# Two masks moved to the start of VectorE's queue, a margin on operand readiness, and a refitted order of issue, in a sliding-window attention plus mixture-of-experts kernel

## The chip, the cores and the metric

The kernel runs on one core of one Trainium2 chip. The metric is the device time of one execution in microseconds (us). The engines are named as in the profile: PE is TensorE's matmul, PEld its weight load, DVE is VectorE, ACT is ScalarE, POOL is GpSimd, SP is SyncE (here it only issues DMAs).

## The reference, cut to what matters

```python
# q, k, v: (B, H, S, D) = (4, 8, 768, 64); n_sink = 4, window = 128
scores = q @ k.T / sqrt(D)
rel = pos[:, None] - pos[None, :]
keep = (pos[None, :] < n_sink) | ((rel >= 0) & (rel < window))
a = softmax(where(keep, scores, -1e9));  attn = a @ v
x = attn.transpose(0, 2, 1, 3).reshape(3072, 512)
p = domain_probs / (domain_probs.sum(-1, keepdims=True) + 1e-9)   # (3072, 4)
out = sum over e in 0..3 of p[:, e:e+1] * (relu(x @ w1[e]) @ w2[e])  # w1: 512 x 1024, w2: 1024 x 512
```

## The kernel before

**Work.** Tokens are handled in 12 pairs of 128-row blocks: batch `b` in 0..3, group `g` in 0..2 (256 rows). Attention for (b, g) has one step per head pair `hp` in 0..3: transposes of q and k (batch 0 on PE, later batches by transposing DMAs on SP's queue), `scores` (L713; it uses 64 rows of the array, two heads side by side), exponentials on ACT (L753), a multiplication by a 0/1 mask on DVE (L734, L763), `values` (L788 for the sink keys, L795 for the window), a reciprocal and a scaling (L822, L825, L834), and for batch 0 a transpose back (`turn`, L856).

The experts' first layer comes in two forms. The dense one (L1109) is 4 groups of 8 matmuls for a unit (b, g, e). The fast one (L1192) is a Strassen-like scheme of seven products P1 to P7, which needs combinations of the tokens (`T`, L1161) and of the weights (L401 to L407), and additions between products on DVE (L1242, L1257) and ACT (L1235, L1248). ReLU and gate are applied by DVE (L1226). The second layer is dense for the first two pairs of batch 0 (`second`, L1436) and also a seven-product scheme for the other ten (`product`, L1361), which needs combinations `S` of the hidden rows (L1307, L1286, called chores) and of `w2` (L366 to L372).

**Order.** There is one instruction stream for each engine, and its order is worked out while the program is built, by a planner inside the kernel function. It keeps a clock for each engine (`t`), predicted ready times for each operand, and a list `pend` of deferred work of ACT, DVE and POOL: `later(engine, ready, slack, run)` puts work there, and among what is ready the one with the earliest `ready + slack` is issued. In each turn of the main loop PE's next step is chosen from `opts`, a list of (ready time, priority, kind):

```python
r, _, kind, step = min(opts, key=lambda o: (o[0] > now + 40, o[0] if o[0] > now + 40 else 0, o[1]))
```

So among the steps that are ready by now + 40 ns the lowest priority number wins, and if none is ready the one that is ready first. If nothing is ready within 220 ns, a product of zeros is issued as a filler (`idle_products`, L581). The priorities: an attention step 0 if due, else 3 (0.1 less for a pair of scores); a fast or dense first-layer step 2 and a little more for the second open unit; opening a unit `OPEN`; a dense second step 1 or `LOW_SECOND`; a product `HIGH_PRODUCT` if DVE's backlog in the planner's clock is over `BEHIND`, else `LOW_PRODUCT`. `SHARE_OF` and `LEAD` say when an attention step is due and when the next batch's attention begins. `LATE1` and `LATE` are added to the time at which a transposing DMA is taken to have landed (batch 1, other batches). `GATE0`, `GATE`, `FORM`, `FORM2`, `TOKEN0`, `TOKEN` are slacks of deferred work, `MARGIN` shortens that of the chores, `WAIT1` and `WAIT2` delay the weights' combinations, `CHORES` is how many chores may be in `pend` at once. `ONLY2` is the first batch for which scores that can come in pairs come only in pairs. `GROW` is the time at which `gates_by_row` (L459 to L465: four DVE operations and a DMA on SP's queue that writes normalised gates to DRAM) is issued. At most `NH` = 6 hidden tiles are live (`mix.live`).

**The masks.** `lent[:, 5*P:10*P]` holds two bias tiles `low` (0 or -32768): the first made by DVE (L536 to L540), the second by ACT (L541, L542). The bias form serves group 0 of batch 0 directly, as an accumulated matmul (L707). The 0/1 masks `mask0` (128 x 384) and `mask1` (128 x 256) are made from them by one DVE `tensor_scalar` each (L550), put into `pend` by `make_mask` with ready time 12000 and slack 8000; `mask_one` (L761) is their first user. The chores of the first product pair wait until the four stores of the dense pairs (`self.stored`) are done in the planner's clock, because `S` reuses the tiles that these stores read.

Of the kernel before, what the change touches and what calls it, by code (L numbers as in the profile page):

```python
# [9 lines left out]
ALU = mybir.AluOpType  # L10
# [6 lines left out]
def kernel(  # L17
# [12 lines left out]
    nc = tc.nc  # L30
# [7 lines left out]
    P = 128  # L38
# [23 lines left out]
    DENSE = 2  # L62
    NT3 = 3
    MIX = 4
    SHARE_OF = (0.712, 1.17, 0.907)
    LEAD = (1.333, 0.307)
    DUE = 0
    LOW_PRODUCT = 2.643
    LOW_SECOND = 4.19
    HIGH_PRODUCT = 0.939  # L70
    EARLY = 0.062
    GATE = 4459
    GATE0 = 1390
    FORM = 17347
    FORM2 = 18856
    TOKEN0 = 0
    WAIT2 = 15161
    WAIT1 = 5608
    LATE3 = 3
    TOKEN = 18312  # L80
    MARGIN = 1544
    FULL = 7
    STEP0 = 0.165
    READY = 54
    WIDE = 2
    OPEN = 1.956
    ONACT = 1
    ONE = 2
    PAIR = 1
    MASKD = 99999999  # L90
    GROW = 29126
    ONLY2 = 2
    BEHIND = 1333
    CHORES = 1
    OWN = 2
    BIASED = 1
    FAST = tuple(START)
# [7 lines left out]
    t = {"pe": 1200.0, "act": 0.0, "dve": 0.0, "pool": 1280.0, "sp": 800.0, "sw": 6500.0, "hw": 0.0}  # L105
    ring, whole = [0.0] * 6, [False] * 6
    WARM = 6600.0
    FLIP = 315
    LATE = 744
    LATE1 = 9766  # L110

    def pe(cols, *deps, n=1, switch=0):
        t["pe"] = max([t["pe"], *deps])
# [11 lines left out]
    def dve(cols, *deps, rate=0.96, fixed=157, shared=None):  # L125
        at = max([t["dve"], *deps])
        if rate == 1.92 if shared is None else shared:
            at += max(0.0, port["pool"] - at - 78)
            port["dve"] = at + fixed + cols / rate
        t["dve"] = at + fixed - 85 + cols / rate  # L130
        return at + fixed + 35 + cols / rate
# [28 lines left out]
    def later(engine, ready, slack, run):  # L160

        pend.append((ready, ready + slack, engine, run))
# [138 lines left out]
    first = {name: sb.tile([P, 2, H, D], BF16, name="qkn", tag="qkn", bufs=NQB) for name in "qk"}  # L301
# [195 lines left out]
    for h in range(H):  # L497
        r = 32 * (h // 2) + NSINK * (h % 2)
        nc.sync.dma_start(
            out=vsf[r:r + NSINK, :, 0:D], in_=v[:, h, 0:NSINK, :].rearrange("b j d -> j b d"),  # L500
# [3 lines left out]
    for sgn in (1, -1):  # L504
        nc.gpsimd.affine_select(
            out=identf, in_=identf, compare_op=ALU.is_ge, fill=0.0,
# [5 lines left out]
    for base, sgn in ((0, 1), (NSINK - 1, -1)):  # L512
        nc.gpsimd.affine_select(
            out=sel2, in_=sel2, compare_op=ALU.is_ge, fill=0.0, base=base,
# [10 lines left out]
    for i in range(1, 4):  # L525
# [7 lines left out]
    two = own[:, None, :].to_broadcast([P, 2, P])  # L533
    LOW = 32768.0
    low = [lent[:, 5 * P:8 * P], lent[:, 8 * P:10 * P]]
    nc.vector.tensor_scalar(  # L536
        out=low[0].rearrange("p (n q) -> p n q", n=3)[:, 0::2], in0=two, scalar1=LOW, scalar2=-LOW, op0=ALU.mult, op1=ALU.add,
# [4 lines left out]
    nc.scalar.activation(out=low[1][:, P:2 * P], in_=own, func=AF.Copy, scale=LOW, bias=-LOW)  # L542
    mask0 = consts.tile([P, 3 * P], BF16, name="mask0")
    mask1 = consts.tile([P, 2 * P], BF16, name="mask1")
    made = []

    def make_mask(i):
        def run(engine):
            x = (mask0, mask1)[i]
            nc.vector.tensor_scalar(out=x, in0=low[i], scalar1=1 / LOW, scalar2=1.0, op0=ALU.mult, op1=ALU.add)  # L550
            dve(4 * P)
            made.append(i)
        later("dve", 12000.0, 8000, run)

    for i in range(2):
        make_mask(i)
    t["dve"] = t["act"] = 4600.0
    cast_first(0)
    flush(4700.0)
# [10 lines left out]
        nc.vector.memset(half[64 * ph:64 * ph + 64, ph:ph + 1], 1.0)  # L570
    for x in ksd:
        nc.vector.memset(x, 0.0)
    t["dve"] += 400.0
    cast_first(1)

# [118 lines left out]
    def scores(b, hp, g, more=False):  # L694
        T = qkT[b]
        w = sum(x[2] for x in GROUPS[g]) * P
        ready = 0.0 if more else scores_ready(b, hp, g)
        slots, sps = [], []
        for ph in range(2):
            i = pick()  # L700
            slots.append(i)
            sps.append(bank(i, [P, 2 * G], FP32, "sps"))
            ring[i] = 1e12
        biased = b == 0 and g < BIASED
        if biased:
            for ph in range(2):
                nc.tensor.matmul(sps[ph][:, 0:w], lhsT=ident, rhs=low[min(g, 1)], start=True, stop=False, skip_group_check=True)  # L707
            pe(2 * w, ready, n=2)
        c = 0
        for (kb, qb, nq) in GROUPS[g]:  # L710
            for ph in range(2):
                pr = slice(64 * ph, 64 * ph + 64)
                nc.tensor.matmul(  # L713
                    sps[ph][:, c:c + nq * P],
                    lhsT=T[pr, 1, hp, kb * P:(kb + 1) * P],
                    rhs=T[pr, 0, hp, qb * P:(qb + nq) * P],
                    start=not biased, stop=True, skip_group_check=biased,
                )
            c += nq * P
        scored_at[b] = done = pe(w, ready, n=6, switch=0 if more else 2)  # L720
        a = sb.tile([P, 2, w], BF16, name="aT", tag="aT", bufs=4)
        m = mask0 if g == 0 else mask1

        def masked(at):
            aT_at[b, hp, g] = at

        if b == 0:
            part = join(2, masked)
        else:
            def mask_both(at):  # L730
                def run(engine):
                    n = 2 if g == 0 else 4
                    x = a if g == 0 else a.rearrange("p h (n w) -> p (h n) w", n=2)
                    nc.vector.tensor_mul(x, x, m[:, None, :].to_broadcast([P, n, 2 * w // n]))  # L734
                    masked(dve(2 * w, rate=1.92))

                def select(engine):
                    x = a.rearrange("p h (n k q) -> p h n k q", n=2, k=2)
                    for k, sgn in ((0, -1), (1, 1)):
                        nc.gpsimd.affine_select(  # L740
                            out=x[:, :, :, k], in_=x[:, :, :, k], compare_op=ALU.is_ge, fill=0.0,
                            base=min(sgn, 0), pattern=[[0, 2], [0, 2], [sgn, P]], channel_multiplier=-sgn,
                        )
                        at = pool(0, fixed=640, shared=True)
                    masked(at + 60)
                if g == 0 or max(t["dve"] - at, 0.0) + 500 * sum(x[2] == "dve" and x[0] < at + 300 for x in pend) < MASKD:
                    later("dve", at, 1500, run)
                else:
                    later("pool", at, 1500, select)
            part = join(2, mask_both)  # L750
        for ph in range(2):
            def run(engine, ph=ph):
                nc.scalar.activation(out=a[:, ph], in_=sps[ph][:, 0:w], func=AF.Exp, scale=scale)  # L753
                at = act(w)
                take(slots[ph], at)
                if b or biased:
                    part(at)
                    return
                assert len(made) == 2

                def mask_one(engine):  # L761
                    x = a[:, ph].rearrange("p (n w) -> p n w", n=2)
                    nc.vector.tensor_mul(x, x, m[:, None, :].to_broadcast([P, 2, 2 * P]))  # L763
                    part(dve(w, rate=1.92))
                later("dve", at, 300, mask_one)
            later("act", done, 300 + 10 * ph, run)
        aTs[b, hp, g] = a
# [700 lines left out]
    mix = Mixture()  # L1468
    att = Attention(0)
# [3 lines left out]
    ahead, upto, loaded, wide = 0, 0.0, 0, 0  # L1473
# [23 lines left out]
    while mix.more() or att.more():  # L1497
        now = t["pe"]
# [19 lines left out]
        x = next((x for x in loads if load_ready(x) < now + 1500), None)  # L1518
# [3 lines left out]
        if turns and (ahead < 2 or not mix.second) and landed.get(("qk", *turns[0]), 1e12) < now and (turns[0][0] <= ahead or turns[0][0] == ahead + 1 and not att.todo):  # L1522
            x = turns.pop(0)
# [10 lines left out]
        next_form()  # L1534
        if ahead + 1 < B and not att.more() and (ahead == 0 or (ahead + 1, 0) in turned_at) and (ahead == 0 or mix.done >= sum(work[:ahead]) * LEAD[ahead - 1]):
            ahead += 1
            att = Attention(ahead)
            upto = mix.done
        share = (sum(work[:ahead]) - upto) * SHARE_OF[max(ahead - 1, 0)]
        due = ahead == 0 or att.steps * share <= (mix.done - upto) * att.total  # L1540
        opts = []
        if att.more():
            opts = [(max(r, now), (DUE if due else 3) - 0.1 * (step == "two"), "att", step) for r, step in att.options()]
        s2, p = mix.second_ready(), mix.product_ready()
        behind = max(t["dve"] - now, 0.0) + 500 * sum(x[2] == "dve" and x[0] < now + 300 for x in pend)
        opts.append((max(p, now), HIGH_PRODUCT if behind > BEHIND or mix.live >= FULL else LOW_PRODUCT, "product", None))
        opts += [(max(f, now), p, "first", x) for f, p, x in mix.firsts()]
        opts.append((max(s2, now), 1 if mix.since >= 1 else LOW_SECOND, "second", None))
        soonest = min(o[0] for o in opts)
        if soonest > now + 40 and flush(soonest, True):  # L1550
            continue
# [3 lines left out]
        if soonest > 1e11:  # L1555
            if loads:
                x = loads.pop(0)
# [4 lines left out]
        r, _, kind, step = min(opts, key=lambda o: (o[0] > now + 40, o[0] if o[0] > now + 40 else 0, o[1]))  # L1562
# [45 lines left out]
```

## Time and profile before

| what | value |
|---|---|
| median of 3 runs | 361.19 us (361.15 to 361.68) |
| the profiled execution: its own time | 362.95 us |
| its span, first to last instruction | 361.2 us |
| granted TensorE clock | 1.000 |
| PE, DVE, ACT, POOL busy | 351.9, 308.8, 169.6, 68.6 us |
| instructions of PE, DVE, ACT, POOL | 4680, 704, 429, 90 |
| fillers (L581), warm-up ones included | 24 |

How to read it: a matmul record includes the pipeline's fill, so "PE busy" says that something was in the array, not that the array was full. Start times of successive matmuls tell more. "Idle before" is the time in which an engine had nothing running ahead of an instruction, with what ended it. The chain is followed back from the last instruction, at each step to what released it.

### The profile page before, as it was taken

Reading aid. Unit: us, or ns where it says so; the run is one execution under the profiler, and the core shown is the slowest. Engines: PE = TensorE matmul, PEld = TensorE weight load, DVE = VectorE, ACT = ScalarE, POOL = GpSimd, SP = SyncE. Lnnn points to the kernel's source line nnn. Section 1 sums busy time; section 2 is a strip of 40 time slices with the busy share of each in tenths; the row PEclk is TensorE's granted clock in tenths of the full one; section 3 lists DMA queues with packets and bytes.
Section 4 is the critical chain, followed back from the end, with each engine's and each line's share of the span. In section 5 each row is a group of like instructions: output and inputs, shape, how many; then the busy total and the mean of one; then the engine's idle time right before and its main releaser. Section 6 shows DMA issues by size and latency. Waiting matters only on the chain.

```text
span 361.2 us, 11129 instructions
## 1 busy us (share of the span) xinstructions
PE 351.9 (97%) x4680; PEld 302.7 (84%) x4680; DVE 308.8 (85%) x704; ACT 169.6 (47%) x429; POOL 68.6 (19%) x90
## 2 busy tenths in 40 slices
PE   8899999999989999999999999999999999999995
PEld 4585788767667999998998998899899999999984
DVE  5869899996979899898898899799898999979740
ACT  5764551567756531536655633952865213222110
POOL 8934015121620712010030610000000000000000
PEclk9999999999999999999999999999999999999999
DMA  9999999999990998661549999131124112000011
GB/s 176 186 193 206 220 222 161 147 172 194 107 176 17 143 193 123 72 89 30 75 75 112 155 130 148 45 75 33 38 68 60 32 31 83 22 31 31 1 60 59
DMA packets 115318, 37.86 MB, mean 105 GB/s; under 512 B 97196, under 2 KB 110764, under 8 KB 115268
## 3 DMA queue, kind: packets, MB, share of 16 engines
q0 software_dynamic: 74416, 17.31, 53.7%
q1 hardware_dynamic: 39796, 19.32, 28.5%
q8 instruction: 36, 0.59, 0.7%
q10 hardware_dynamic: 1056, 0.52, 0.5%
q14 instruction: 14, 0.11, 0.1%
HBM read 41.03 MB, written 6.34 MB: 131 GB/s over the span
## 4 chain that ended last, share of the span: by engine, by line
PE 77%; DVE 13%; DMA 5%; issue 2%; ACT 1%; POOL 1%; DVEq 0%; ACTq 0%
PE cps L1192 32%; PE acc L1361 29%; PE acc L1436 6%; DVE H L1226 3%; PE hps L1109 3%; PE od L795 2%; PE sps L713 2%; DMA xT<-onat 2%; DMA vx<-in_v_dram 2%; DVE H L1257 1%; DMA out_dram<-osb 1%; DVE T L1161 1%; DVE S L1307 1%; PE od L788 1%; DVE cps L1242 1%
## 5 line engine op out<-in xcount | busy, mean ns | idle before, releaser
L1192 PEld LDWEIGHTS <-w 128*128 128x128 bf16 x1408 | 87.6, 98 | 4.6 <-issue 1.3
L1361 PEld LDWEIGHTS <-H 128*128 128x128 bf16 x720 | 66.2, 98 | 7.4 <-issue 1.1
L1226 DVE SCALAR_TENSOR_TENSOR H<-cps,gates 128x512 bf16<-128x512 f32 x105 | 70.3, 680 | 1.2 <-issue 0.7
L1361 PE MATMUL acc<-w,H 128*128 128x256 bf16 x432 | 58.5, 273 | 0.1
L753 ACT ACTIVATE aT<-sps 128x512 bf16<-128x512 f32 (+1 forms) x96 | 47.0, 574 | 18.2 <-PE sps L713 18.1
L1192 PE MATMUL cps<-T,w 128*128 128x128 bf16 x704 | 53.6, 219 | 0.3 <-DVE cps L1242 0.3
L1192 PE MATMUL cps<-xT,w 128*128 128x128 bf16 x704 | 52.3, 219 | 0.1
L1235 ACT COPY cps<-cps 128x512 f32<-128x512 f32 x44 | 25.5, 581 | 42.8 <-PE cps L1192 38.7
L1408 ACT COPY osb<-acc 128x256 f32<-128x256 f32 x40 | 15.2, 380 | 61.0 <-PE acc L1361 56.8
L834 ACT ACTIVATE onat<-od,R 128x64 bf16<-128x64 f32 x144 | 33.4, 331 | 20.1 <-DVE R L822 20.0
L1361 PE MATMUL acc<-wf,H 128*128 128x256 bf16 x288 | 38.8, 273 | 0.0
L1242 DVE TENSOR_TENSOR cps<-H,cps 128x512 f32<-128x512 f32 x40 | 27.6, 690 | 9.8 <-PE cps L1192 6.7
L1192 PEld LDWEIGHTS <-qkn 128*128 128x128 bf16 x576 | 34.7, 98 | 1.0 <-issue 0.5
L1361 PEld LDWEIGHTS <-S 128*128 128x128 bf16 x320 | 29.7, 98 | 5.6 <-DVE S L1307 1.7
L328 POOL DMA_DIRECT2D vx<-in_v_dram x24 | 21.4, 902 | 55.3 <-PE od L795 45.5
L1436 PE MATMUL acc<-w,H 128*128 128x512 bf16 x128 | 30.3, 379 | 0.0
L1192 PEld LDWEIGHTS <-vf 128*128 128x128 bf16 x480 | 29.1, 98 | 0.9 <-issue 0.3
L1248 ACT COPY H<-cps 128x512 f32<-128x512 f32 x40 | 23.7, 593 | 11.5 <-PE cps L1192 11.4
L1257 DVE TENSOR_TENSOR H<-H,cps 128x512 f32<-128x512 f32 x40 | 27.1, 677 | 1.5 <-PE cps L1192 1.4
L1192 PE MATMUL cps<-T,qkn 128*128 128x128 bf16 x384 | 27.0, 219 | 0.1
L734 DVE TENSOR_TENSOR aT<-aT,mask 128x1024 bf16<-128x1024 bf16 (+1 forms) x36 | 22.7, 637 | 4.7 <-ACT aT L753 4.7
L268 POOL DMA_DIRECT2D rows<-in_q_dram x18 | 16.1, 892 | 45.9 <-DMA qkT<-rows 26.8
(124 smaller groups left out, 529.6 us busy)
## 6 DMA issues: line engine op xcount, KB each, us to landing
w<-in_moe_w_dram POOLq DMA_DIRECT2D x7, 1024.0 KB, 21.1
out_dram<-osb SPq DMA_DIRECT2D x23, 256.0 KB
gates<-gate_rows SPq DMA_DIRECT2D x40, 128.0 KB
vx<-in_v_dram POOLq DMA_DIRECT2D x24, 128.0 KB, 7.5
rows<-in_q_dram POOLq DMA_DIRECT2D x18, 128.0 KB, 7.5
rows<-in_k_dram POOLq DMA_DIRECT2D x18, 128.0 KB, 7.2
w<-in_moe_w_dram POOLq DMA_DIRECT2D x4, 256.0 KB, 8.4
kraw<-in_k_dram ACTq DMA_DIRECT2D x2, 256.0 KB
```

What stands on the lines that cost most here:

```text
L328: nc.gpsimd.dma_start(out=vx[tb][:, :, 0:D], in_=v[b, :, tb * P:(tb + 1) * P, :].rearrange("h p d -> p h d"),)
L734: nc.vector.tensor_mul(x, x, m[:, None, :].to_broadcast([P, n, 2 * w // n]))
L753: nc.scalar.activation(out=a[:, ph], in_=sps[ph][:, 0:w], func=AF.Exp, scale=scale)
L834: nc.scalar.mul(o[:, qi, hp, ph * D:(ph + 1) * D], od[:, qi, ph, 0:D], R[:, qi, ph])
L1192: nc.tensor.matmul(y[:, f], lhsT=A[:, d, f * P:(f + 1) * P], rhs=T[:, d], start=(m in ("P1", "P5") and f == 0 and d == 0), stop=(d == 1), ...
L1226: nc.vector.scalar_tensor_tensor(out=dst, in0=src, scalar=0.0, in1=gate, op0=ALU.max, op1=ALU.mult)
L1235: nc.scalar.copy(out=tiles["Y"], in_=y)
L1242: nc.vector.tensor_add(tiles["V"], c5, tiles["X"])
L1248: nc.scalar.copy(out=c5, in_=y)
L1257: nc.vector.tensor_add(c5, c5, y)
L1361: nc.tensor.matmul(x, lhsT=self.operand(b, g, e, m)[:, f], rhs=forms[e][m][:, f], start=(k == 0 and f == 0 and m in (("P1", "P5", "P2") if ...
L1436: nc.tensor.matmul(op, lhsT=H[:, fb // QF, fb % QF, s], rhs=w2_sb[e][:, fb, :], start=(fb == 0), stop=(fb == NFB - 1),)
```

## The change

The two mask operations leave the planner's deferred list and are issued at a fixed place: on DVE right behind the zeroing of `ksd` (L572), which in DVE's stream is ahead of the first cast of the loaded rows (L299). `PAD`, 200 ns, is added to the planner's ready time of a product always, and of attention, first-layer and dense second steps once batch 1's attention has begun (`ahead > 0`). Twenty-six constants get other values. By the code, two of them cannot alter an order: `READY` is not read, and `FULL` is compared with `mix.live`, which stays at 6 or less.

```diff
-    SHARE_OF = (0.712, 1.17, 0.907)
-    LEAD = (1.333, 0.307)
+    SHARE_OF = (0.635, 1.148, 0.943)
+    LEAD = (1.227, 0.235)
...
-    LOW_PRODUCT = 2.643
-    LOW_SECOND = 4.19
-    HIGH_PRODUCT = 0.939
-    EARLY = 0.062
-    GATE = 4459
-    GATE0 = 1390
-    FORM = 17347
-    FORM2 = 18856
-    TOKEN0 = 0
-    WAIT2 = 15161
-    WAIT1 = 5608
+    LOW_PRODUCT = 2.816
+    LOW_SECOND = 4.296
+    HIGH_PRODUCT = 0.403
+    EARLY = 0.138
+    GATE = 5742
+    GATE0 = 5043
+    FORM = 19230
+    FORM2 = 38137
+    TOKEN0 = 220
+    WAIT2 = 19401
+    WAIT1 = 6201
...
-    TOKEN = 18312
-    MARGIN = 1544
-    FULL = 7
-    STEP0 = 0.165
-    READY = 54
+    TOKEN = 11696
+    MARGIN = 828
+    FULL = 8
+    STEP0 = 0.155
+    READY = 39
...
-    OPEN = 1.956
+    OPEN = 1.336
...
+    PAD = 200
...
-    GROW = 29126
-    ONLY2 = 2
-    BEHIND = 1333
-    CHORES = 1
+    GROW = 22996
+    ONLY2 = 1
+    BEHIND = 6520
+    CHORES = 3
...
-    FLIP = 315
-    LATE = 744
-    LATE1 = 9766
+    FLIP = 179
+    LATE = 2342
+    LATE1 = 12449
...
-    made = []
-
-    def make_mask(i):
-        def run(engine):
-            x = (mask0, mask1)[i]
-            nc.vector.tensor_scalar(out=x, in0=low[i], scalar1=1 / LOW, scalar2=1.0, op0=ALU.mult, op1=ALU.add)
-            dve(4 * P)
-            made.append(i)
-        later("dve", 12000.0, 8000, run)
-
-    for i in range(2):
-        make_mask(i)
...
     for x in ksd:
         nc.vector.memset(x, 0.0)
+    for x, y in zip((mask0, mask1), low):
+        nc.vector.tensor_scalar(out=x, in0=y, scalar1=1 / LOW, scalar2=1.0, op0=ALU.mult, op1=ALU.add)
     t["dve"] += 400.0
     cast_first(1)
...
-                assert len(made) == 2
-
...
-            opts = [(max(r, now), (DUE if due else 3) - 0.1 * (step == "two"), "att", step) for r, step in att.options()]
+            opts = [(max(r + PAD * (ahead > 0), now), (DUE if due else 3) - 0.1 * (step == "two"), "att", step) for r, step in att.options()]
...
-        opts.append((max(p, now), HIGH_PRODUCT if behind > BEHIND or mix.live >= FULL else LOW_PRODUCT, "product", None))
-        opts += [(max(f, now), p, "first", x) for f, p, x in mix.firsts()]
-        opts.append((max(s2, now), 1 if mix.since >= 1 else LOW_SECOND, "second", None))
+        opts.append((max(p + PAD, now), HIGH_PRODUCT if behind > BEHIND or mix.live >= FULL else LOW_PRODUCT, "product", None))
+        opts += [(max(f + PAD * (ahead > 0), now), p, "first", x) for f, p, x in mix.firsts()]
+        opts.append((max(s2 + PAD * (ahead > 0), now), 1 if mix.since >= 1 else LOW_SECOND, "second", None))
```

## The prediction, made before the changed kernel was run

> **What bounds the kernel now.** I read the page first, then the stages, then the chain of waits in the stretches where PE loses time.
>
> ```profile
> PE 351.9 (97%) x4680; PEld 302.7 (84%) x4680; DVE 308.8 (85%) x704; ACT 169.6 (47%) x429; POOL 68.6 (19%) x90
> ```
>
> PE is the bound, and it has little left to lose. From the chain's pieces, 16 matmuls of L1192 take 0.89 us (56 ns each), 12 of L1361 1.31 (109 ns), 8 of L1436 1.73 (216 ns), 8 of L1109 0.87 (109 ns). Times the page's counts: 2464 x 0.056 + 1120 x 0.109 + 128 x 0.216 + 128 x 0.109 = 302 us; attention, transposes and fillers, worked out the same way from their chain pieces, are some 38 more. PE thus has about 340 us of work, none of which the change removes except fillers. The first matmul starts at 1.4 us, the span is 361.2, and some 4 us at the end are the last store: about 16 us in all can be won, and no more. Where they lie, by stages (PE's busy time is the second number of a row, DVE's the fourth):
>
> ```profile
> 5.00:10.00 5.00, 4.68 (x45) 2.65 (x45) 2.15 (x7) 3.91 (x10) 5.00 (x7) 1.00 1.95 193
> 10.00:15.00 5.00, 4.35 (x72) 2.76 (x69) 4.14 (x12) 3.20 (x8) 4.53 (x10) 1.00 1.83 179
> 15.00:20.00 5.00, 4.53 (x68) 3.33 (x68) 4.49 (x15) 4.49 (x10) 4.47 (x6) 1.00 1.38 201
> ...
> 40.00:60.00 20.00, 20.00 (x220) 15.33 (x219) 18.72 (x36) 7.55 (x14) 4.84 (x6) 1.00 1.44 207
> 60.00:80.00 20.00, 19.95 (x267) 15.97 (x266) 19.77 (x37) 11.66 (x23) 6.54 (x8) 1.00 1.79 157
> ...
> 100.00:150.00 50.00, 48.35 (x669) 43.51 (x668) 44.54 (x109) 23.15 (x63) 11.57 (x14) 1.00 1.24 129
> ```
>
> PE is idle at the start and just after 100 us; from 40 to 80 it is full, with DVE nearly so (38.5 of 40 us). In the first stretch the chain runs through DVE:
>
> ```profile
> 3.51 5.83 DMA vx<-in_v_dram
> ...
> 12.74 0.57 DVE mask L550
> 13.31 0.09 DVE R L822
> 13.41 0.02 issue
> 13.43 0.42 DVE onat L825
> 13.85 1.19 DVE mask L550
> 15.04 0.20 DVE xT L299
> 15.24 0.60 DVE qkT L299
> ```
>
> The load of the first values releases it at 9.34 us; from then to 17.8 nearly every piece is DVE's, and both masks are in it. PE meanwhile issues fillers (five at 11.89, four at 16.83) and waits.
>
> **The change part by part.**
>
> *Masks.* Away from 12.74 and 13.85: 0.57 + 1.19 = 1.76 us of DVE in the chain. What is next late: R at 13.23 needs the values that end at 12.78, so 0.4 us is won there and onat ends at about 13.4; then the transpose of 13.91 and its copy (now 15.04) come 0.45 us earlier by data, the copy about 1.2, the qkT copy 1.1. After that PE needs rows and first weights; the first quarter of w was issued at 7.13 with 8.4 us to landing, so the dense step of 15.95 can't begin before about 15.5. I take 1.1 us of the 1.76; bounds 0 and 1.76.
> At the new place the rows show a hole:
>
> ```profile
> 3.64 0.19 DVE L572 MEMSET ksd<- 128x64 uint32 x2
> 4.51 0.43 DVE L299 CAST qkn<-qraw 128x512 bf16<-128x512 f32 x1 [0.69 <-DMA qraw<-in_q_dram]
> ```
>
> The nearest operations of the kind took 0.23 us (L536, 128x256) and 0.19 (L539, 128x128), so about 0.25 + 0.23 = 0.5 us, which the 0.69 us wait for the rows covers. The added wait is on ACT's L542, which ends at 3.74, before DVE is there; queued behind it is only that cast. If both cost what they did (1.76), the cast ends at 6.0 instead of 4.94; the k cast on ACT ends at 5.58 anyway, so 0.4 would be lost. Value 0.
> Why mask1 took 1.27 us for 256 columns and mask0 0.65 for 384: POOL's L652 ran from 13.90 to 14.95, and mask1 ended at 15.04. The Trainium skill (SBUF — State Buffer, "SBUF: two separate sides") states that VectorE and GpSimd share an exclusive port, held for a whole instruction, so that the other blocks; the trace agrees here. By that rule masks at 3.8 us would hold up POOL, which is then writing the second values' load; this is a rival below.
>
> *Priorities.* Only their ranks count. LOW_PRODUCT stays between 2.2 and 2.9, HIGH_PRODUCT between 0 and 1, LOW_SECOND over 3, OPEN between 1 and 2, EARLY and STEP0 only break ties as before. With READY and FULL, seven numbers change nothing: 0.
>
> *Scores in pairs from batch 1 on (ONLY2).* In the timeline a pair (12 matmuls of L713) occupies 0.62 us, a single (6) 0.40: the pair saves 0.18. Between 76 and 117 us there are eight singles, at 76.5, 78.6, 92.5, 97.5, 111.3, 112.6, 114.0 and 116.3; as four pairs they save 0.7. A pair wants four of six banks at once and may come later: -0.5, bounds -0.7 and 0.
>
> *GROW.* The four gate operations (0.17 + 0.52 + 0.32 + 0.32 in the chain, 30.07 to 31.47) lie ahead of vf and qkT on DVE, and PE then waits 0.23 us twice at 32.4 and 33.4. Issued some 6 us earlier they meet a DVE that idles 2.2 us until 26.98. Their DMA on SP's queue goes with them; SP waits 23.0 us for it already and passes nothing. -0.4, bounds -0.8 and 0.
>
> *PAD, LATE, LATE1.* The waits of PE after 95 us that a 200 ns margin can remove are those for DVE's cps and H, 0.3 + 0.2 + 0.2; where another step is ready the margin costs nothing. -0.3, bounds -0.7 and +0.4 (four fillers of 0.11 us, as at 16.83, where no other step is ready).
>
> *The stall at 100 us.* This is the largest wait left:
>
> ```profile
> 96.24 4.25 DMA out_dram<-osb
> 100.48 0.10 DVE R L822
> 100.58 1.99 issue
> 102.58 0.42 DVE S L1307
> ```
>
> The S tiles reuse the rows of the last dense store. The chore is issued to DVE before the store is done, DVE's queue stands 2.0 us, with all behind it, and PE loses 0.58 + 0.52 in the waits that the trace names and 0.4 more at 108. The change leaves the planner's price of a store alone; PAD covers 0.2 of 2.0. Where the order puts the store and the chore can't be told from this trace: 0, bounds -1.5 (gone) and +1.5 (a second engine-long stand of the same size, as three chores may now be out at once).
>
> *The rest (slacks, SHARE_OF, LEAD, BEHIND).* They move steps, not work. I value them at 0, with the bounds that the rivals give.
>
> Sum: -1.1 - 0.5 - 0.4 - 0.3 = -2.3; 0.3 is taken off for what is hidden by loads. So -2.0 on the profiled 362.95, which is 0.5% over the median; on the median 359.2.
>
> **Rivals.**
> 1. *DVE becomes the bound (slower).* BEHIND goes from 1333 to 6520, so PE is no longer turned to products, which need little of DVE, when DVE is 1.3 us late, and first-layer units follow each other. By rows a fast unit costs DVE 3 x 0.68 + 0.69 + 0.68 + 4 x 0.42 = 5.1 us against 56 matmuls x 56 ns = 3.1 of PE; only the products (28 x 109 ns) make that 6.2. For it: DVE is at 38.5 of 40 us from 40 to 80. Against: six hidden tiles bound how far units run ahead, and a unit that isn't ready still gives way. It decides once two units in a row are common. At 0.08 us of wait for each of the 44 fast units (a wait of 0.2 to 0.3, as the trace's single ones, at every third unit), +3.5 - 2.0: 362.7.
> 2. *The start's gain is hidden.* DMA is at 9 tenths or more until 100 us; if weights decide when batch 0 goes on, the masks and GROW bring nothing: -0.8, and less with one new wait: 360.8.
> 3. *The store's stall goes too.* -2.0 - 1.5: 357.7.
> 4. *POOL held up by the masks.* The second values' load lands up to 0.5 us later, straight into the chain at 9.34: -2.0 + 0.5: 359.7. Against: the first such load beside L536 and L539 took 0.98 us where the mean is 0.90. By the skill's lock, the same +0.5.
> 5. *Order hardly altered.* The masks leave and nothing else falls into place: -0.5 to -1: within 2's time.
>
> **Numbers.** Chances: forecast 0.42, rival 1 0.26, 2 and 5 together 0.17, 3 0.10, 4 0.05. About 0.2% (0.7 us) is what a measurement of this kernel can tell from no change. Faster takes the forecast, 3, 4 and a little of 2: 0.58; same 0.14; slower 0.28. The range goes from 357.0 (3 with its bounds) to 363.5 (nearly all of 1); the forecast's own is 357.7 to 360.4.
>
> **What would show it.** Right: no L550 after 5 us, the masks at about 0.25 us each before the first cast; the xT copy of 15.04 near 14; fewer than 15 fillers after 6 us; only pairs of 12 (or 8) in L713 of batch 1; L459 near 24 us; products beginning about a microsecond or two before 96.96. Wrong: PE waits for "DVE H" or "DVE cps" that sum to over 3 us after 100, DVE at 48 of 50 us in a stretch with PE under 49, or a "DVE S" wait after a store that is longer than 2 us.

## The result, and the profile after

Faster by 0.5%: the ratio of after to before is 0.9951, 95% interval 0.9936 to 0.9965. Medians over 22 runs each are 362.40 us before and 360.73 after; the profiled execution after took 360.94 us with a span of 359.2. The runs of before lie between 360.61 and 365.02 us, those of after between 360.32 and 361.19: in these 22 executions each, the new order varies much less.

Two stages of the kernel before, and then the stages of the kernel after, PE's busy time second and DVE's fourth in a row:

```profile
20.00:25.00 5.00, 5.00 (x61) 4.17 (x59) 4.44 (x18) 2.62 (x6) 0.52 (x1) 1.00 1.43 198
...
80.00:100.00 20.00, 20.00 (x250) 13.78 (x248) 16.52 (x33) 14.25 (x44) 8.06 (x10) 1.00 1.50 151
```

```profile
10.00:15.00 5.00, 4.68 (x85) 3.18 (x81) 3.83 (x11) 3.69 (x9) 4.33 (x9) 1.00 1.83 179
...
20.00:25.00 5.00, 4.17 (x53) 3.44 (x52) 4.65 (x20) 2.47 (x5) 0.47 (x1) 1.00 1.43 199
...
80.00:100.00 20.00, 19.00 (x240) 13.22 (x238) 16.20 (x31) 15.44 (x42) 5.06 (x7) 1.00 1.47 170
100.00:150.00 50.00, 49.50 (x710) 45.17 (x707) 46.17 (x115) 26.70 (x78) 15.18 (x18) 1.00 1.33 128
150.00:200.00 50.00, 50.00 (x733) 45.95 (x731) 46.49 (x104) 26.42 (x76) 6.13 (x7) 1.00 0.56 71
```

PE gains 0.3 us between 10 and 15 and 1.2 between 100 and 150, but it loses 0.8 between 20 and 25 and 1.0 between 80 and 100, where it was full before. Busy time hides the small waits, so the same is set out below from the starts of successive matmuls: the time from one start to the next, less the matmul's own time (128, 256 or 512 columns at 56, 109 and 216 ns, scores at half because two heads run side by side; fillers count as waiting).

| stretch, us | beyond the matmuls' own time, before | after |
|---|---|---|
| 0 to 20 | 9.2 | 8.2 |
| 20 to 40 | 1.5 | 2.5 |
| 40 to 80 | 0.8 | 0.3 |
| 80 to 100 | 1.0 | 2.5 |
| 100 to 120 | 3.1 | 1.0 |
| 120 to the end | 3.6 | 2.5 |
| sum | 19.2 | 17.0 |

The last matmul starts at 357.16 us before and at 355.18 after. So the 2.0 us are a balance: 1.0 at the start, 2.1 at 100 to 120, 0.5 at 40 to 80 and 1.1 after 120, against 2.5 lost at 20 to 40 and 80 to 100; 0.2 goes into one more auxiliary matmul of 512 columns. DVE's timeline of the kernel after, the masks and the first cast:

```profile
4.18 0.33 DVE L563 TENSOR_SCALAR mask<-lent 128x384 bf16<-128x384 bf16 x2
4.49 0.87 DVE L300 CAST qkn<-qraw 128x512 bf16<-128x512 f32 x1
```

Both masks together take 0.33 us here, in the hole where they were put. In the other six profiles with the masks at this place (e1, e4, e7, e8, e9, e11) they take 0.71 us, from 3.74 on. And DVE's timeline where it stood for 2.0 us before, at the first `S<-S,H` (the chores are written S0 below for `S<-H` and S1 for `S<-S,H`; it is at S1 that DVE stood for the last dense store):

```profile
100.44 0.74 DVE L1296 TENSOR_TENSOR S<-H 128x512 bf16<-128x512 bf16 x2
101.14 0.18 DVE L811 RECIPROCAL R<-od 128x4 f32<-128x4 f32 x1
101.24 0.26 DVE L1150 TENSOR_TENSOR T<-xT,T 128x256 bf16<-128x256 bf16 x1
101.42 0.69 DVE L725 TENSOR_TENSOR aT<-aT,mask 128x1024 bf16<-128x1024 bf16 x1
102.02 0.42 DVE L1296 TENSOR_TENSOR S<-H 128x512 bf16<-128x512 bf16 x1
102.35 0.28 DVE L1150 TENSOR_TENSOR T<-xT 128x256 bf16<-128x256 bf16 x1
102.55 0.28 DVE L1150 TENSOR_TENSOR T<-xT,T 128x256 bf16<-128x256 bf16 x1
102.76 0.42 DVE L1296 TENSOR_TENSOR S<-S,H 128x512 bf16<-128x512 bf16 x1
```

The last row shows no idle time. The last dense store was issued at 97.40, 5.4 us earlier; before, DVE arrived 4.3 us after the store, and it now has other work in between. The distance is not all of it: before, the store was done 6.3 us after its issue, so here it must also have landed at least 0.9 us sooner. PE's largest waits for other engines in the kernel after (us in total, times, longest):

```profile
PE acc L572 <- DVE lent L494: 1.4, 1, 1.4
PE tx L845 <- DVE onat L814: 1.1, 3, 0.7
PE acc L1350 <- ACT acc L1379: 0.5, 1, 0.5
PE cps L1181 <- DVE cps L1231: 0.5, 1, 0.5
PE sinks L665 <- DVE qkT L300: 0.4, 1, 0.4
PE sps L704 <- ACT aT L744: 0.3, 1, 0.3
```

All of them lie before 102 us; after that, by the starts of successive matmuls, PE has a single hole of over 0.15 us, at 332 us.

### The profile page after: what moved, and what is told of

The parts are those of the page before. It is cut to its first block, busy times and chain, and to the rows that moved or that the text cites. A ratio compares the mean times of both kernels' runs of the same rounds, so it can differ in the third digit from the quotient of the medians.

```text
span 359.2 us, 11107 instructions
## 1 busy us (share of the span) xinstructions
PE 349.9 (97%) x4678; PEld 302.7 (84%) x4678; DVE 309.0 (86%) x703; ACT 168.6 (47%) x430; POOL 68.9 (19%) x90
## 4 chain that ended last, share of the span: by engine, by line
PE 86%; DMA 6%; ACT 3%; DVE 2%; issue 1%; POOL 1%; SPq 0%; ACTq 0%; DVEq 0%
PE cps L1181 38%; PE acc L1350 34%; PE acc L1425 6%; DMA vx<-in_v_dram 3%; PE sps L704 2%; PE od L784 2%; PE hps L1098 2%; DMA kraw<-in_k_dram 2%; DMA scratch<-in_moe_domain_probs_dram 1%; ACT onat L823 1%; ACT aT L744 1%; PE od L777 1%; DVE aT L752 0%; DVE onat L814 0%; DVE osb L1435 0%
## 5 line engine op out<-in xcount | busy, mean ns | idle before, releaser
L1181 PEld LDWEIGHTS <-w 128*128 128x128 bf16 x1408 | 86.3, 98 | 3.2 <-issue 0.8
L1350 PE MATMUL acc<-w,H 128*128 128x256 bf16 x432 | 57.5, 273 | 0.5 <-ACT acc L1379 0.5
L1181 PE MATMUL cps<-T,w 128*128 128x128 bf16 x704 | 52.5, 219 | 0.5 <-DVE cps L1231 0.5
L1237 ACT COPY H<-cps 128x512 f32<-128x512 f32 x40 | 23.4, 593 | 19.3 <-PE cps L1181 19.2
L1215 DVE SCALAR_TENSOR_TENSOR H<-H,gates 128x512 bf16<-128x512 f32 x35 | 23.9, 685 | 0.0
```

Source lines behind the costliest of these rows:

```text
L1181: nc.tensor.matmul(y[:, f], lhsT=A[:, d, f * P:(f + 1) * P], rhs=T[:, d], start=(m in ("P1", "P5") and f == 0 and d == 0), stop=(d == 1), ...
L1215: nc.vector.scalar_tensor_tensor(out=dst, in0=src, scalar=0.0, in1=gate, op0=ALU.max, op1=ALU.mult)
L1237: nc.scalar.copy(out=c5, in_=y)
L1350: nc.tensor.matmul(x, lhsT=self.operand(b, g, e, m)[:, f], rhs=forms[e][m][:, f], start=(k == 0 and f == 0 and m in (("P1", "P5", "P2") if ...
```

## The experiments

Four runs (e1 to e4) keep the order on every engine and the planner's clocks as they were and move one thing on DVE alone; e5 keeps the order and leaves a store out; e11 moves work from ACT to DVE under an unchanged order of PE. In these (in e11 up to the first instruction that ACT lacks) the same instruction of ACT can be compared by its number, which shows at what time a gain arises and whether it lasts. The others set one constant and let the planner make a new order. The edits are shown shortened.

A ratio is taken to executions of before that ran beside the run; their medians were 362.61 us for e1 to e4, 363.55 for e5 to e8 and 362.88 for e9 to e12. The kernel after ran only beside the 362.40 of the result. A distance of e7, e8, e9 or e11 from the kernel after therefore comes out otherwise by the times than by the ratios, by up to 1.1 us, and both are given.

**Masks early, nothing else (e1).** The planner still charges its clock where it did; only the instruction moves.

```diff
-            nc.vector.tensor_scalar(out=x, in0=low[i], ...)      # in make_mask
             dve(4 * P)
...
+    for x, y in zip((mask0, mask1), low):                        # behind the zeroing of ksd
+        nc.vector.tensor_scalar(out=x, in0=y, ...)
```

> The kernel before with its order of issue unchanged on every engine, except that the two mask operations are issued on DVE right after L572. Theory A (prediction): the 1.76 us of masks leave DVE's chain and PE keeps about 1.1 us of it to the end: ratio about 0.997. Theory B (the start's gain is given back at the next thing that comes late before 30 us): the scores of 18.0 us come about 1 us earlier, but the end moves by 0.3 us or less: ratio 0.999 to 1.000. Theory C (POOL and DVE hold each other up at 4 us): masks over 0.5 us each or the first load on POOL later, and values later than 9.4 us: ratio above 1.000.

Measured: ratio 0.9986 (0.9962 to 1.0010), 362.37 us. The interval holds A's 0.997 and B's 1.000, so the traces have to decide. By the same ACT instructions this run is 0.2 us behind the profile of before at 8 us (the first values land when they land), 0.7 ahead at 18, 0.9 ahead from 36 to 100, and 2.4 after 104, where the store landed early; 0.6 is lost again after 220. The instruction of ACT just ahead of the stall, from the timelines of before, of e1, of e2 and of e5 in this order:

```profile
100.07 0.44 ACT L1390 COPY acc<-acc 128x256 f32<-128x256 f32 x1
```
```profile
99.20 0.45 ACT L1391 COPY acc<-acc 128x256 f32<-128x256 f32 x1
```
```profile
99.72 0.45 ACT L1388 COPY acc<-acc 128x256 f32<-128x256 f32 x1
```
```profile
99.37 0.44 ACT L1390 COPY acc<-acc 128x256 f32<-128x256 f32 x1
```

The last of these is e5, where nothing ahead of 90 us was changed, and yet it is 0.7 early. Of e1's 0.9, then, at most 0.7 (by 18 us) belongs to the masks, and against e5 it is 0.3 at 18 us and 0.2 at 99. Theory B's "given back before 30 us" is wrong in this order: what is won at 18 us is still there at 100. Theory C is wrong too. But A's 1.1 is too much, for a reason that the masks' own rows in DVE's timeline show (before; then e5, with the same instructions in the same order):

```profile
12.66 0.65 DVE L550 TENSOR_SCALAR mask<-lent 128x384 bf16<-128x384 bf16 x1
13.77 1.27 DVE L550 TENSOR_SCALAR mask<-lent 128x256 bf16<-128x256 bf16 x1
```
```profile
12.77 0.25 DVE L550 TENSOR_SCALAR mask<-lent 128x384 bf16<-128x384 bf16 x1
13.48 0.30 DVE L550 TENSOR_SCALAR mask<-lent 128x256 bf16<-128x256 bf16 x1
```

POOL's L652 began at 13.90 in the one and at 14.41 in the other. The masks cost 0.55 us, or 1.9 where POOL's load of q (from 12.38) and then L652 run beside them; in e5 that load began at 12.88, after the first mask, and L652 0.6 us after the second had ended. Nothing in the order differs between the two, so which of them happens depends on the execution.

**Gate operations early, nothing else (e2)**, the kernel before with `gates_by_row` at 23 us and the planner's charge left at 29.

```diff
-        if not gated_rows and (loaded or GROW and now > GROW):
+        if not gated_rows and now > 22996:
             gated_rows.append(1); gates_by_row()
+        if not charged and now > 29126:
+            charged.append(1); dve(600, 0.0); sp(t["dve"])
```

> The kernel before with its order unchanged, except that the four gate operations of DVE and their DMA are issued at about 23 us, not 30. Theory A (prediction): they sat in DVE's chain ahead of the qkT copy; PE gains 0.4 us (0 to 0.8): ratio 0.999. Theory B: they hold up the last scaling (onat) of the second group at 23 us, or nothing that PE waits for at 32 us moves: 0 or +0.3 us.

Measured: ratio 0.9990 (0.9971 to 1.0008), 362.38 us. That is A's number, but the interval holds 1 as well; the trace decides. The ACT instructions run 0.05 us ahead up to 34 us and 0.35 from 36 on; but e5, without any change there, gains the same 0.3 at the same place. What differs there is the gate operation L460: it took 0.51 us in the profile of before and 0.18 to 0.30 in e2, e1 and e5. So the move itself is worth about nothing in this order: B.

**Masks late in the kernel after (e3).** `make_mask` put back without its charge.

> The kernel after with its order unchanged, except that the two mask operations are issued on DVE where the planner's clock reaches 12 us, as before. Theory A: the mirror of the first run, +1.1 us on the kernel after, ratio to before about 0.998. Theory B: +0.3 or less, ratio about 0.996.

Measured: ratio 0.9949 (0.9932 to 0.9967), 360.72 us, which is the kernel after's 360.73. The same ACT instructions are 0.21 us late at 16.6 and level from 22 to 80 us. B. The masks took 0.75 us here, and by 22 us both kernels wait for the same scaling (`onat`; in the kernel after it is the 0.7 in L845's row above). PE's timeline of e3 has it at the same time:

```profile
22.99 0.29 PE L853 MATMUL tx<-ident,onat 128*128 128x128 bf16 x2 [0.66 <-DVE onat L822]
```

**Gate operations late in the kernel after (e4).**

> The kernel after with its order unchanged, except that the four gate operations are issued at about 29 us, as before. Theory A: +0.4 us on the kernel after. Theory B: no change or a gain of up to 0.3 us, because the waits for onat at 22 us and for qkT at 31 us do not come from them.

Measured: ratio 0.9982 (0.9963 to 1.0000), 361.92 us, 1.2 over e3, which ran beside it, and over the kernel after. The ACT instructions are 0.35 late at 31 us (this run's start) and 1.33 from 34 on. The chain is plain in the timelines of DVE and of PE, with PE's row of the kernel after last:

```profile
30.76 0.25 DVE L460 TENSOR_REDUCE scratch<-scratch 128x24 f32<-128x96 f32 x1
31.04 0.18 DVE L461 TENSOR_SCALAR scratch<-scratch 128x24 f32<-128x24 f32 x1
31.25 0.30 DVE L462 RECIPROCAL scratch<-scratch 128x24 f32<-128x24 f32 x1
31.59 0.32 DVE L463 TENSOR_TENSOR scratch<-scratch 128x96 f32<-128x96 f32 x1
31.83 1.28 DVE L300 COPY qkT<-tr 128x512 bf16<-128x512 bf16 x2
```
```profile
32.56 0.40 PE L702 MATMUL sps<-qkT 64*128 64x128 bf16 x6 [1.18 <-DVE qkT L300]
```
```profile
31.23 0.40 PE L704 MATMUL sps<-qkT 64*128 64x128 bf16 x6 [0.19 <-DVE qkT L300]
```

PE waits 1.18 us for a copy behind them, where the kernel after waits 0.19. A, and more than its 0.4: in the new order PE reaches these scores without a dense step in between.

**The store left out (e5)**, the kernel before without the store of rows 384 to 511 of the output.

```diff
-                    nc.sync.dma_start(out=out[r:r + P, :], in_=dst)
+                    if (g, s) != (1, 1):
+                        nc.sync.dma_start(out=out[r:r + P, :], in_=dst)
```

> The kernel before with its order unchanged, leaving out one 256 KB store (rows 384 to 511 of the output, the last dense one), so that the S tiles don't wait for it. Theory A: the stand of DVE at 100.6 us (2.0 us) costs PE about 1.5 us that nothing else would cost: ratio 0.996, and the runs lie closer together than those of before, whose scatter of over 3 us comes from when this DMA lands. Theory B: PE would wait at 102 to 108 us for DVE anyway, or the scatter comes from other DMAs: 0.3 us or less, scatter as before.

Measured: ratio 0.9953 (0.9924 to 0.9981), 361.60 us. From ACT's copy at 99.37 to its next copy of a result into the output tile `osb` 2.5 us pass, in the profile of before 4.5: there the stand costs 2.1 us, A's price and more. It is not the same in every execution: DVE stood 2.0 us in the profile of before, but 1.36 in e2 and 0.39 in e1, whose order is the same at this place. A's second half fails: the runs still lie between 359.65 and 364.01 us, so this store is not what makes before scatter. DVE's timeline without the wait:

```profile
99.36 0.42 DVE L1307 TENSOR_TENSOR S<-H 128x512 bf16<-128x512 bf16 x1
99.69 0.18 DVE L822 RECIPROCAL R<-od 128x4 f32<-128x4 f32 x1
99.81 0.42 DVE L1307 TENSOR_TENSOR S<-S,H 128x512 bf16<-128x512 bf16 x1
```

**Pairs alone (e6): ONLY2 = 1 in before; and the kernel after with ONLY2 = 2 (e8).**

> The kernel before with ONLY2 = 1 alone; the order is as before up to the first scores of batch 1 (76 us) and replanned after. Theory A (prediction): only pairs in batch 1, eight singles less, 0.7 us less of PE time and -0.5 at the end: ratio 0.9985. Theory B: the replanned order moves other waits by more than that, ratio anywhere within 0.5% of 1, and the trace shows the 0.1 us per pair beside larger changes.

> The kernel after with ONLY2 = 2. Theory A: singles come back in batch 1, +0.5 us on the kernel after: ratio to before 0.9965. Theory B: replanning decides: ratio 0.993 to 1.000, with the change of PE's waits larger than 0.7 us.

Measured: e6 369.55 us, ratio 1.0154 (1.0122 to 1.0185), slower by far more than either theory allowed. In e6 PE waits 3.3 us for DVE's additions of partial sums (cps, L1242), the last dense store leaves at 101.38 instead of 96.24, and DVE stands for it (e6's waits from 78 to 112 us: who waited for whom, us in total, times, longest):

```profile
DVE S L1307 <- DMA out_dram<-osb: 4.3, 1, 4.3
...
PE cps L1192 <- DVE cps L1242: 3.3, 2, 2.0
```

e8 took 361.29 us, ratio 0.9938 (0.9915 to 0.9960): 0.56 us over the kernel after by the time, and 0.5 under it by the ratio. So even the sign of the singles' price is not settled. e8 also loses the waits at 97 to 101 us and has some 0.6 us more of others between 80 and 95 (three matmuls whose records are missing taken off), so the pairs are not isolated by it. The price of a pair is seen directly: from its first start to the next step a pair takes 0.55 us and a single 0.33, so four pairs in place of eight singles save 0.4 us and what the eight changes of shape cost the step ahead.

**No margin (e7): PAD = 0 in after; and the margin alone (e12): PAD = 200 in before.**

> The kernel after with PAD = 0. Theory A (prediction): the margin is worth 0.3 us; waits of 0.2 to 0.4 us of PE for DVE come back after 100 us: ratio to before 0.996. Theory B (the margin is what empties PE's waits after 105 us): 1 us or more, ratio 0.998 or above, with five or more waits over 0.15 us after 105 us where the kernel after has one. Theory C: no loss, ratio 0.995.

> The kernel before with the 200 ns margin alone. Theory A (prediction): -0.3 us, ratio 0.999. Theory B (the constants are fitted together; a margin alone replans from 13 us on and the stand at the store falls where it may): ratio outside 0.997 to 1.003, decided at 80 to 110 us.

Measured: e7 372.79 us, ratio 1.0254 (1.0224 to 1.0284), 11 to 12 us over the kernel after; e12 368.23 us, 1.0149 (1.0118 to 1.0180). Without the margin the new constants give the slowest order of all, and the margin without the new constants is slow too. DVE's timeline in e7, the stand at the store at its longest:

```profile
104.51 0.39 DVE L1296 TENSOR_TENSOR S<-H 128x512 bf16<-128x512 bf16 x1
109.12 0.42 DVE L1296 TENSOR_TENSOR S<-S,H 128x512 bf16<-128x512 bf16 x1 [4.21 <-DMA out_dram<-osb]
```

PE waits 4.0 us for that one, and 1.4 and 0.9 us for DVE's cps and ACT's onat. More is lost right behind the stand: in e7's trace the granted TensorE clock is 0.69 from 110 to 112 us, 0.50 from 112 to 114 and 0.96 from 114 to 116, where the other stretches of 2 us around it have 1.00. Worked out from these three figures that is some 1.7 us. It follows PE's longest wait of all the profiles; that the wait causes it is not shown. So A is wrong. B's size is reached, but not its kind: about half of what comes back is the store's stand and the low clock behind it, and after 120 us the trace has only two waits of PE of over 0.15 us, the longer one 0.24.

In e12 DVE stands 3.9 us at the store, and PE waits 2.3 us for DVE's cps, most of it behind that stand, and 1.7 for ACT's osb copy. Twelve of the eighteen executions of e6, e10 and e12 had a mean clock of 0.991 to 0.995, those in the kept traces 0.999 or 1.000. So their medians hold a loss of clock too, and no trace shows where it falls.

**The number of chores: CHORES = 1 in after (e9), CHORES = 3 in before (e10).**

> The kernel after with CHORES = 1. Read from the runs so far: the last dense store takes 4.7 to 8.9 us from its issue, DVE stands at the first S1 (S<-S,H) until it lands, and the kernel after has three S0 (S<-H) ahead of the first S1, before one. Theory A: three chores at once are what covers the store; with one, the stand of 1 to 4 us comes back at the first S1 and the time is 1 to 3 us over the kernel after, ratio 0.998 to 1.003. Theory B: the distance from the last store to the first S1 is set by the rest of the order; no stand, ratio 0.994 to 0.996.

> The kernel before with CHORES = 3 alone. Theory A: the first S1 comes at least 5 us after the last store, the stand at 100 us goes, -1.5 us or more: ratio 0.996 or less. Theory B (it helps only with the other constants): the replanned order has a stand of its own, ratio 1.000 to 1.015.

Measured: e9 362.68 us, ratio 0.9992 (0.9978 to 1.0006), 1.5 us over the kernel after by the ratio and 1.95 by the time; e10 369.18 us, 1.0167 (1.0141 to 1.0194). The theory of how the store is covered (A) falls in both, although e9's ratio lies where A put it. In e9 the first S1 comes after a single S0, at 101.86, and DVE doesn't stand; the time is lost after 260 us (PE holes of 0.41 us at 275 and 0.75 at 310). In e10 three S0 come first, and DVE stands 1.3 us all the same; 3.1 us more are PE's waits for a masked aT. So three chores neither cover the store nor are needed for it. What does cover it is not isolated: in e9 DVE reached S1 4.8 us after the store's issue and found it done, in e10 (as before) it was done only after 6.3. How long the store takes counts beside DVE's order.

**Scalings on DVE (e11)**, a try to better the kernel after: the sixteen scalings of batch 1, group 0 leave ACT.

```diff
+            if (b, g) == (1, 0):       # behind the reciprocal; ACT's four multiplications left out
+                nc.vector.tensor_mul(o[:, :, hp]..., od[:, :, :, 0:D], R.to_broadcast([P, 2, 2, D]))
```

> The kernel after with PE's, POOL's and SP's order unchanged; the sixteen scalings of batch 1, group 0 (92.8 to 96.1 us on ACT, 3.3 us) are done by DVE, one 128x256 operation of 0.42 us for each head pair, behind its reciprocal. Theory A: ACT's chain of 92 to 101 us (scalings, then exponentials, then the seed copy) is what PE waits for at 97.3, 97.6, 98.2 and 100.9 us, 1.7 us in all: -1.0 to -1.7 us on the kernel after, ratio 0.991. Theory B: the added 1.7 us of DVE delay the store's last addition or the masks as much: 0 or slower.

Measured: ratio 0.9964 (0.9942 to 0.9986), 361.75 us, 1.0 over the kernel after by the time and 0.5 by the ratio. The holes at 97 to 101 us are 0.27, 0.46, 0.30, 0.46 and 0.25 us, against 0.29, 0.46, 0.30 and 0.67: nearly the same but for the last, so ACT's scalings did not cause the first four. What did was not found. No run beats the kernel after by more than its scatter.

**A second stand.** Ten of the fourteen profiles, before and after included, have ACT stand for an output store of the product phase, because its next copy goes into the one `osb` tile. ACT's rows near 220 us in after, e4 and e11, and the line of e12's waits:

```profile
221.10 0.37 ACT L1397 COPY osb<-acc 128x256 f32<-128x256 f32 x1 [3.46 <-DMA out_dram<-osb]
```
```profile
224.06 0.65 ACT L1395 COPY osb<-acc 128x256 f32<-128x256 f32 x2 [5.31 <-DMA out_dram<-osb]
```
```profile
223.02 0.65 ACT L1403 COPY osb<-acc 128x256 f32<-128x256 f32 x2 [5.64 <-DMA out_dram<-osb]
```
```profile
ACT osb L1409 <- DMA out_dram<-osb: 6.4, 1, 6.4
```

At 3.5 us PE loses nothing; at 5.3, 5.6 and 6.4 it has holes of 1.07, 1.40 and 1.89 us. In e4 and e11 the order around it is the kernel after's, so the order is not what makes the difference. That it varies between executions of one kernel, and so makes part of the scatter, is likely but not shown, as each kernel left one trace.

## Why the prediction was right, and where it was not

The forecast was -2.0 us, 359.2 on the 361.19 then known, a ratio of 0.9945; measured 0.9951, and the spans differ by 2.0. The direction and the size came out. The working behind them did so only in part. The time of 360.73 itself is over the forecast's own 357.7 to 360.4, because before, with 22 runs, has its median at 362.40 and not at 361.19.

- *What bounds it.* Right. PE's columns are the same but for one auxiliary matmul, and gains that have reached 40 us last: in the runs of unchanged order they stand to a hundredth or two of a microsecond from 40 to 80 us. That refutes rival 2 for before's order. In the new order half of it came true: the masks' gain is hidden by 22 us (e3), though by a wait for DVE's scaling and not for weights; that of GROW is not (e4).
- *Masks, -1.1: mis-sized.* In before's order they are worth 0.3 to 0.7 us at 18 us, in after's order nothing (e3). The step that failed is taking 0.57 + 1.19 as a price that DVE would save in any execution, when without POOL's work beside them the two cost 0.55 (e5); and taking what is won at 15 us as won, when by 22 us the new order waits for the scalings. The 0.5 us for the new place was right in kind (0.33 in the kernel after, 0.71 in e1), and the wait for the rows covered it.
- *Rival 4, POOL held up.* Not seen: POOL's two value loads took 1.93 us with the masks beside them (e1) and 1.92 without (e2, e5). It went the other way round: POOL held DVE. POOL's load of q in before and in the kernel after:

```profile
4.38 1.03 POOL L258 DMA_DIRECT2D qkn<-in_q_dram  x1
```
```profile
4.21 0.90 POOL L259 DMA_DIRECT2D qkn<-in_q_dram  x1
```

The first cast took 0.43 us where this load took 0.96 to 1.09 (before, e2, e3, e6, e7), and 0.72 to 0.89 where it took 0.88 to 0.90 (the other nine): in all fourteen profiles one of the two pays. That fits the exclusive port that the Trainium skill describes (SBUF — State Buffer, "SBUF: two separate sides"), with either side as the loser.
- *Priorities, 0.* Right: with LOW_PRODUCT, LOW_SECOND, HIGH_PRODUCT, EARLY, STEP0, OPEN, READY and FULL at their old values the changed kernel has the same instructions in the same order on all five engines. (They are eight; "seven" was a miscount.)
- *Pairs, -0.5.* Right in mechanism: no singles are left in batch 1. The 0.7 behind it was too large, because it was worked out from the rows' durations, which include the pipeline's fill; by starts it is 0.4. No run isolates it (e8).
- *GROW, -0.4: mis-sized, and reasoned from an order in which it is worth nothing.* In before's order it gains nothing (e2), in the new one 1.0 to 1.2 us (e4). Of the two short waits at 32 us that the prediction blamed on the gates, the first stays in e2 without them; the second is gone in e2, but also in e1 and e5, where the gates stand as before.
- *PAD, -0.3: the step failed.* It was priced as an edit that takes away small waits. It is one term of a fit: without it the other constants give 11 to 12 us more than the kernel after (e7), and alone it makes before 1.5% slower (e12).
- *The stall at 100 us, 0: mis-sized.* In the profiled executions it costs 2.1 us (e5) and is gone, the largest single gain; rival 3 gave it 1.5 and a chance of 0.10. Why it is gone is known only in part: measured from the store's issue DVE arrives 1.0 us later, and the store was done sooner.
- *The rest, 0.* This hides the losses that made the sum come out: 1.0 us more waiting at 20 to 40 and 1.5 more at 80 to 100.
- *Rival 1, DVE as the bound.* Not seen: after 105 us the kernel after has one PE hole of over 0.15 us, and its +3.5 us needed some fifteen waits of 0.2 to 0.3. DVE reached 46.5 of 50 us.
- *The signs.* The first product came at 96.50 instead of 96.96, 0.5 us earlier and not one or two: the new waits at 20 to 40 and 80 to 100 had eaten into the start's gain by then. Fewer than 15 fillers after 6 us could show nothing, since before had 11 there (after: 7).

So the right total is in good part luck: terms of -1.1 and -0.3 that were not there in that form stood in for a stall of -2 that was priced at 0 and for new waits of +2.5.

## What to carry to other kernels

Where a planner's constants are fitted together, a change can't be priced constant by constant: each of three constants moved alone (e6, e10, e12) cost 1.5 to 1.7%, and the whole change won 0.5%. Freeze the order and move one instruction to learn what that instruction costs; compare the same instruction by its number in both traces, and compare also two executions that should be alike, which showed here that 0.7 us at 99 us is the scatter of the start. Among waits, look first for an in-order engine that stands at a tile whose old contents a DMA is still reading: DVE stood so in all four slow replans, 1.3 us in e10 and 3.9 to 4.3 in e6, e7 and e12.

## What the runs showed of the hardware that was not expected

A 256 KB store on SP's queue beside transposing DMAs and POOL's loads was done 4.7 to 8.9 us after its issue (4.7 in e1, 6.3 before, 6.0 in e6, 8.9 in e7, by the first S1 that waited for it). In before's order alone it took 4.7 (e1), 5.7 (e2) and 6.3 us. The same mask operation took 0.30 us in e5, where POOL's L652 began 0.6 us after its end, and 1.27 us before, where L652 ran beside it. Behind a 4.0 us wait of PE the granted clock was 0.69, then 0.50 for 2 us each (e7).
